# Windowed attention and a gated MLP on one core: six of nine token groups in blocks of two, the MLP's first product there by seven products of sums

## The chip, the cores and the metric

The kernel runs on one core of one Trainium2 chip. The metric is the device time of one execution in microseconds (us); lower is better. The engines are PE (matrix products), DVE (vectors), ACT (scalar functions and copies), POOL (a second, slower vector engine) and SP (issues nearly all the DMA transfers here). PE reads its operands from SBUF and writes to eight banks of PSUM, each of 128 partitions by 512 fp32.

## The reference

Eight batches, eight heads, 576 tokens, 64 values a head. Heads 0 to 3 attend to the last 32 tokens, heads 4 to 7 to every fourth of the last 128. The result, 4608 tokens by 512, goes through a gated MLP.

```python
scores = scale * np.matmul(q, k.transpose(0, 1, 3, 2))
scores = np.where(masks, scores, -1e9)          # window 32, or 32 of dilation 4
attn = exp(scores - max(scores)); attn = attn / (sum(attn) + 1e-9)
x = matmul(attn, v)                             # (B, S, H*D) -> 4608 x 512
h = x @ w_in                                    # 512 x 2048
g = h * (1.0 / (1.0 + np.exp(-1.702 * h)))
out = g @ w_out                                 # 2048 x 512
```

## The kernel before, in words

Every operand of the MLP's products is held as two fp32r parts, a high one and a low one; a product is three matmuls (high by high, low by high, high by low) of a 128x128 weight tile (stationary) by 128 x 512 tokens (moving). The weights arrive as 64-bit numbers and are decoded once on the chip: `decode(n)` fetches one of 32 tiles (16 of w_in, 16 of w_out) into one of five buffers called cells (L307, on SP's queue), and ACT, DVE and POOL turn it into a high and a low part (L311 to L321; the low part is a subtraction, L269). The names are wih, wil, woh and wol.

The tokens are worked through in nine groups of 512: m0 to m6 are the first 512 tokens of batches 0 to 6, r is the last 64 tokens of all eight batches, m7 the first 512 of batch 7; r comes before m7. For each group the MLP goes over 16 tiles f of d_ff. `up(f)` is the first product of one tile: 12 matmuls into one PSUM bank, hp (L631). Then ACT takes a tanh from the bank (L639), DVE multiplies it with the bank (the gate, L642), ACT copies the high part gh (L262) and DVE subtracts to get the low part gl (L269). `down(f)` is the second product of the tile, 12 matmuls (L667, L668, L671) into four banks acc0 to acc3, which hold the group's output over all 16 tiles. The second product of a tile follows the first product of the next, so the way from bank to gh and gl lies under matmuls.

Attention is done by head pairs, four to a batch, 32 in all, numbered k. A head pair is: scores on PE into the two banks sp (L408), mask, maximum and subtraction on DVE, exponential on ACT, sum and reciprocal on DVE, normalisation on POOL, transposes on DVE, eight copies into bt, then the product with v on PE (L509) into the bank av and the free end of sp, and copies from there into xm (the group's tokens) and xr (the rests). From the eighth head pair on the scores of the next pair and the product of this one are one piece on PE. The head pairs of a batch run while the group of the batch before is in the MLP. The first four run ahead of everything, and decoding runs through m0's stage.

No queue is written by hand. Each operation is added to a plan with its estimated cost on each engine that may do it, an urgency, and the names that it reads and writes; `Plan.ordered` then walks through estimated time and fixes the order on PE, ACT, DVE, POOL and SP's queue. An engine runs its instructions in that order, and so does SP's queue of transfers, where a transfer that waits for its data holds those behind it.

Of the kernel before, what the change touches and what calls it, by code (L numbers as in the profile page):

```python
# [7 lines left out]
F32 = mybir.dt.float32  # L8
# [13 lines left out]
LT = S - GT  # L22
AHEAD = 0.58
# [4 lines left out]
QT = 5  # L28
# [3 lines left out]
ROW = S // 4  # L32

# [130 lines left out]
def tile_windowed_attention_then_gated_mlp(  # L164
# [16 lines left out]
    ps = ctx.enter_context(tc.tile_pool(name="ps", bufs=1, space=bass.MemoryType.PSUM))  # L181
    plan = Plan()
# [14 lines left out]
    wih = fixed([P, NF, NC, P], F32R, "wih")  # L197
    wil = fixed([P, NF, NC, P], F32R, "wil")
    woh = fixed([P, NF, DM], F32R, "woh")
    wol = fixed([P, NF, DM], F32R, "wol")  # L200
    xh = fixed([P, NC, GT], F32R, "xh")
    xl = fixed([P, NC, GT], F32R, "xl")
    ghs, gls = ([fixed([P, GT], F32R, f"{n}{j}") for j in range(2)] for n in ("gh", "gl"))
    xm = fixed([P, NC, GT], F32, "xm")
    xr = fixed([P, B, NC, LT], F32, "xr")
# [29 lines left out]
    early = temp([P, GT], F32, "g32", "early")  # L235
# [32 lines left out]
    def pair(e, dst, a, b, op):  # L268
# [3 lines left out]
    second = fixed([P, 2, DM], U64, "second")  # L272
    cells = [temp([P, DM], U64, "ost", "cell0"), temp([P, DM], U64, "ost2", "cell1"), fixed([P, DM], U64, "cell2"),
             second[:, 0], second[:, 1]]
    words = fixed([P, 3, DM], U32, "words")

    def decode(n, urgency):
# [9 lines left out]
        if n % 2:  # L287
            src, hi, lo, key = w_out[f], woh[:, f], wol[:, f], f"wo{f}"
        else:
            hi, lo = (w[:, f].rearrange("p c n -> p (c n)") for w in (wih, wil))  # L290
            src, key = w_in[f], f"wi{f}"
# [37 lines left out]
    late, main_x, left_x = (t.rearrange(f"p {' '.join(d)} -> p ({' '.join(d)})") for t, d in (  # L329
        (second.bitcast(F32), "jn"), (xm, "cn"), (xr[:, 1:], "bcn")))  # L330
    nv = NW * D
    late_v = words.bitcast(F32).rearrange("p j n -> p (j n)")
# [4 lines left out]
    def lots(k):  # L337

        if 0 < k < NC:
            return f"first qk{k}", f"first v{k}"  # L340
        return ("qk0", "v0") if k < FIRST * NC or k % 2 == 0 else ("qk1", "v1")

    def load_qk(k):
        u, place = pairs[k], lots(k)[0]

        def work(e):
            if 0 < k < NC:
                flat = (None, late, main_x, left_x)[k]
            else:
                flat = late if place == "qk1" else temp([P, 2 * S], F32, "qk", f"qk_{k}")  # L350

            u["qk"] = flat[:, 0:2 * S]
            load(u["qk"], qk[k])
# [3 lines left out]
    def load_v(k):  # L357
        u, place = pairs[k], lots(k)[1]

        def work(e):  # L360
# [7 lines left out]
            flat = late_v if place == "v1" else temp([P, 2 * nv], F32, "v", f"v_{k}")  # L368
# [7 lines left out]
    def waits(k):  # L376

        if k >= FIRST * NC and k % 2:
            return [f"w{x}{f}" for x in "io" for f in range(NF - 3, NF)]
        return ["xh3.0"] if NC <= k < FIRST * NC else []  # L380
# [29 lines left out]

    def exponentials(k, urgency):
# [8 lines left out]
        if not masked(k):  # L420
            mine = mask if dilated(k) else plain
            for n, tiles, cost in ((P, slice(0, QT - 1), 0.62), (D, slice(QT - 1, QT), 0.22)):
                add({DVE: cost}, urgency, lambda e, n=n, tiles=tiles: pair(
                    e, pr[0:n, :, tiles], u["all"][0:n, :, tiles],
                    mine[0:n, None, tiles].broadcast_to([n, 2, tiles.stop - tiles.start, W]), ALU.add),
                    ("sp",), (PR,))
# [73 lines left out]
    def product(k):  # L500
        u = pairs[k]
        u["av"] = bank([P, GT], "av", f"av_{k}")
        sp = pairs[k + 1]["sp"] if k + 1 < len(pairs) else bank([P, 2, GT], "sp", f"sp_{k + 1}")
        u["rest"] = sp[:, 1, QT * W:QT * W + LT]
# [6 lines left out]
    def drain_x(k, urgency):  # L511
# [19 lines left out]
        if b == 0:  # L531
# [13 lines left out]
            for n, (part, src) in enumerate(rests):  # L545
                add({ACT: 0.22, DVE: 0.2}, urgency, lambda e, part=part, src=src: copy(e, part(xr[:, b, c]), src()),
                    FOUR, (f"xr{b}{c}.{n}",))
            return
        banks = ("av", "left")
        for n, (size, part, src, other) in enumerate(mains):  # L550
            place = banks[other]
            add({ACT: 0.12 + size * 0.001}, urgency, lambda e, part=part, src=src: copy(
                e, part(view(xm[:, c])), src()), (place,), (f"xm{c}.{n}", *freed))
        for n, (part, src, other) in enumerate(rests):
            add({ACT: 0.22, DVE: 0.2}, urgency, lambda e, part=part, src=src: copy(
                e, part(view(xr[:, b, c])), src()), (banks[other],),
                (f"xr{b}{c}.{n}", *(("first v3", "first qk3") if b == 1 else ())))
# [14 lines left out]
    def attention(k, urgency):  # L572


        def alone(j):
            add({PE: 1.6}, urgency - 1.0e5, lambda e: scores(j), (lots(j)[0], *(["mask"] if dilated(j) else [])), ("sp", "left", f"scores{j}"), 1.0)

        if k == NC:
# [3 lines left out]
        more, apart = k + 1 < len(pairs), k + 1 <= FIRST * NC  # L582
# [3 lines left out]
        if apart:  # L586
# [7 lines left out]
        ready = [f"scores{k + 1}"] if apart else [lots(k + 1)[0]] if more else []  # L594
        add({PE: 1.2 if apart or not more else 2.3}, urgency - 1.0e5, work,
            (lots(k)[1], *(f"bt.{m}" for m in range(8)), *ready), ("left", "av", *([] if apart else ["sp"])), 1.0)
        drain_x(k, urgency)

    class Group:


        def __init__(self, name, keys, dest):
            self.name, self.keys, self.dest = name, keys, dest
            self.g, self.acc, self.hps = {}, {}, {}
# [203 lines left out]
```

## Time and profile before

| | |
|---|---|
| median of 3 runs | 891.64 us (890.78 to 891.83) |
| span of the profiled execution | 888.8 us (the page gives no other time of it) |
| instructions | 17107, of them 7304 on PE |
| PE busy | 875.5 us, 99% of the span |
| DVE, ACT, POOL busy | 445.3, 392.4, 94.1 us |
| DMA | 61.32 MB, 69 GB/s on average |

The page is read from the busy times to the chain that ended last: the work followed back from the last instruction, at each step to what released it. In the rows of groups a form such as `hp_m<-xh,wih` names the tile written and the tiles read; m stands for any main group. In rows of a timeline a bracket at the end gives the idle time of the engine before the instruction, and what ended it. A matmul's duration in a timeline (0.39 us) is longer than its share of PE, because matmuls overlap; the distance between starts is what it costs. The rows are in the prediction.

### The profile page before, as it was taken

How to read it: one execution, taken by the hardware profiler on the slowest of the kernel's cores; microseconds unless marked ns; L12 is line 12 of the kernel's file. 1: busy time of each engine (PE TensorE's matmuls, PEld its weight loads, DVE VectorE, ACT ScalarE, POOL GpSimd, SP SyncE). 2: the span in 40 equal slices, each digit the busy share in tenths (PEclk: the TensorE clock that was granted, in tenths of full speed). 3: DMA queues.
4: the chain of work that ended last, by engine and by line, in shares of the span. 5: the costliest groups of instructions: out<-in, count | busy, mean ns of one | idle time of the engine just before them, and what ended most of it. 6: DMA issues, size and time to landing. Idle time of an engine off the chain costs nothing.

```text
span 888.8 us, 17107 instructions
## 1 busy us (share of the span) xinstructions
PE 875.5 (99%) x7304; PEld 715.8 (81%) x7304; DVE 445.3 (50%) x808; ACT 392.4 (44%) x687; POOL 94.1 (11%) x105
## 2 busy tenths in 40 slices
PE   6999999999999999999999999999999999999998
PEld 4678788888888888888888888888888888888886
DVE  6898986565556245543564265624522322232222
ACT  7898864443544245333543254424522332232222
POOL 3352331010101000000010010100100000000000
PEclk9899999999999999999999999999999999999999
DMA  9467752311231012200411023100100010002001
GB/s 360 149 204 227 223 140 95 94 48 47 96 94 48 0 56 87 88 8 0 142 47 48 1 95 94 48 1 26 44 1 1 0 48 1 1 0 48 1 1 47
DMA packets 35803, 61.32 MB, mean 69 GB/s; under 512 B 17424, under 2 KB 17680, under 8 KB 35728
## 3 DMA queue, kind: packets, MB, share of 16 engines
q1 hardware_dynamic: 35584, 60.11, 20.9%
q8 instruction: 57, 0.93, 0.5%
q14 instruction: 18, 0.15, 0.1%
q10 hardware_dynamic: 144, 0.13, 0.0%
HBM read 49.48 MB, written 9.44 MB: 66 GB/s over the span
## 4 chain that ended last, share of the span: by engine, by line
PE 97%; ACT 1%; DMA 1%; issue 0%; DVE 0%; SPq 0%
PE hp_m L631 40%; PE acc_m L667 13%; PE acc_m L671 13%; PE acc_m L668 13%; PE hp_r L631 5%; PE av L509 3%; PE sp L408 3%; PE acc_r L668 2%; PE acc_r L667 2%; PE acc_r L671 2%; DMA cell<-wo_dram 1%; PE first_x L495 1%; PE sp L509 0%; ACT cell L311 0%; ACT words L317 0%
## 5 line engine op out<-in xcount | busy, mean ns | idle before, releaser
L631 PE MATMUL hp_m<-xh,wih 128*128 128x512 f32 x512 | 202.2, 395 | 0.0
L667 PE MATMUL acc_m<-gh,woh 128*128 128x512 f32 x512 | 200.6, 392 | 0.0
L631 PE MATMUL hp_m<-xl,wih 128*128 128x512 f32 x512 | 199.7, 390 | 0.4 <-DVE xl L269 0.4
L631 PE MATMUL hp_m<-xh,wil 128*128 128x512 f32 x512 | 199.8, 390 | 0.0
L668 PE MATMUL acc_m<-gh,wol 128*128 128x512 f32 x512 | 199.3, 389 | 0.0
L642 DVE SCALAR_TENSOR_TENSOR g_m<-g_m,hp_m 128x512 f32<-128x512 f32 x128 | 87.7, 686 | 214.4 <-ACT g_m L639 213.4
L639 ACT ACTIVATE g_m<-hp_m 128x512 f32<-128x512 f32 x128 | 76.8, 600 | 234.3 <-PE hp_m L631 233.8
L671 PE MATMUL acc_m<-gl,woh 128*128 128x512 f32 x512 | 142.5, 391 | 0.0
L269 DVE TENSOR_TENSOR gl<-g_m,gh 128x512 fp32r<-128x512 f32 x126 | 92.5, 734 | 61.3 <-ACT gh L262 59.2
L631 PEld LDWEIGHTS hp_m<-xh,wih 128*128 128x128 f32 x512 | 96.4, 188 | 21.3
L631 PEld LDWEIGHTS hp_m<-xl,wih 128*128 128x128 f32 x512 | 96.4, 188 | 21.2 <-DVE xl L269 0.9
L667 PEld LDWEIGHTS acc_m<-gh,woh 128*128 128x128 f32 x512 | 96.1, 188 | 20.6
L262 ACT ACTIVATE gh<-g_m 128x512 fp32r<-128x512 f32 x126 | 79.8, 633 | 73.3 <-DVE g_m L642 73.1
L668 PEld LDWEIGHTS acc_m<-gh,wol 128*128 128x128 f32 x512 | 96.1, 188 | 19.6
L631 PEld LDWEIGHTS hp_m<-xh,wil 128*128 128x128 f32 x512 | 96.4, 188 | 19.1
L671 PEld LDWEIGHTS acc_m<-gl,woh 128*128 128x128 f32 x512 | 95.5, 188 | 20.1
L269 POOL TENSOR_TENSOR pr<-pr,sm 128x320 f32<-128x320 f32 x64 | 49.4, 793 | 312.5 <-DVE sm L437 312.5
L262 ACT ACTIVATE bt<-ct 32x320 f32<-32x320 f32 x100 | 46.9, 469 | 5.1 <-DVE ct L458 3.2
L262 ACT ACTIVATE xm<-av 128x512 f32<-128x512 f32 (+2 forms) x42 | 24.5, 592 | 47.6 <-PE av L509 25.1
L269 POOL TENSOR_TENSOR xl<-xm,xh 128x512 fp32r<-128x512 f32 x10 | 13.8, 1394 | 260.0 <-ACT xh L262 256.3
L431 ACT ACTIVATE pr<-pr 128x640 f32<-128x640 f32 x32 | 23.7, 740 | 29.2 <-DVE pr L269 29.0
L642 DVE SCALAR_TENSOR_TENSOR g_r<-g_r,hp_r 128x512 f32<-128x512 f32 x16 | 11.0, 688 | 49.7 <-ACT g_r L639 49.7
(125 smaller groups left out, 850.7 us busy)
## 6 DMA issues: line engine op xcount, KB each, us to landing
qk<-qk_dram SPq DMA_DIRECT2D x17, 576.0 KB, 4.5
out_dram<-ost_m SPq DMA_DIRECT2D x31, 256.0 KB, 2.1
second<-qk_dram SPq DMA_DIRECT2D x13, 576.0 KB, 4.3
v<-vp_dram SPq DMA_DIRECT2D x32, 216.0 KB, 4.5
words<-vp_dram SPq DMA_DIRECT2D x24, 216.0 KB, 4.4
cell<-wi_dram SPq DMA_DIRECT2D x10, 512.0 KB, 4.7
cell<-wo_dram SPq DMA_DIRECT2D x9, 512.0 KB, 4.7
second<-wo_dram SPq DMA_DIRECT2D x6, 512.0 KB, 4.9
```

The costliest lines, as they stand in the source:

```text
L262: A.activation(dst, src, AF.Copy, scale=scale)
L269: (V if e == DVE else G).tensor_tensor(out=dst, in0=a, in1=b, op=op)
L408: T.matmul(dst[:, w:w + n], u["qk"][rows, at:at + 32], u["qk"][rows, S + first:S + first + n], start=not masked(k), stop=True, tile_positi ...
L431: add({ACT: 0.75}, urgency, lambda e: A.activation(prs[y], prs[y], AF.Exp, scale=0.125), (), (PR,))
L495: T.matmul(u["x"][D * a:D * a + D, g, at:to], u["v"][32 * g:32 * g + 32, s - 1 if dilated(k) else s, a], ct[32 * g:32 * g + 32, a, n:n + t ...
L509: T.matmul(dst, u["v"][a][0:KW, m], bt[0:KW, a, m], start=True, stop=True, skip_group_check=True)
L631: T.matmul(hps[f], st[:, f, c], mv[:, c], start=c == 0 and k == 0, stop=c == NC - 1 and k == 2)
L639: A.activation(self.g32, hps[f], AF.Tanh, scale=0.851)
L642: V.scalar_tensor_tensor(out=self.g32, in0=self.g32, scalar=1.0, in1=hps[f], op0=ALU.add, op1=ALU.mult)
L667: T.matmul(self.acc[j], woh[:, f, cols], gh, start=f == 0, stop=False)
L668: T.matmul(self.acc[j], wol[:, f, cols], gh, start=False, stop=False)
L671: T.matmul(self.acc[j], woh[:, f, P * j:P * j + P], self.g[f][1], start=False, stop=f == NF - 1)
```

## The change

Groups m0, m1 and m2 stay as they were. The other six are taken in three blocks of two: p (batches 3 and 4), q (batches 5 and 6) and r (the rests, then batch 7).

In a block, two tiles of d_ff, f = u and f = u + 8, are made together for both groups: a 2 by 2 block product over the two halves of d_model, by the scheme of Strassen in the form with seven products. With weights' sums (index b) and tokens' sums (index a) the seven are listed in `PRODUCTS`; each is 6 matmuls (two chunks of d_model by three parts). They alternate between the banks hp and av; some of them are added up in PSUM, three results are copied out to SBUF and come back as an addition on DVE. The first group's gated tiles are multiplied with w_out at once, in 16 pieces spread between the seven products of the next pair; the second group's are kept in SBUF, and their 16 steps of the second product come after the block's eight pairs (`rest`).

- Weights' sums: `sum_weights(u)` makes four sums for each pair u, with high and low parts, and writes them and three plain parts to DRAM (`sums`, 56 tiles of 256 KB). Every product of every block loads its tile into one of eight slots (168 loads of 256 KB).
- Tokens' sums: tokens of batches 3 to 7 and the rests are written to DRAM (L587, L599) and loaded per block (L842, eight tiles); `sum_tokens` adds and splits them, and the parts take the place of w_in in SBUF.
- w_out of f from 9 on is written to DRAM once (`outs`, 7 tiles of 512 KB) and loaded again in turns (18 loads).
- Buffers: cells, tokens, gated values and output tiles share an array of 22 units, `arena`. Attention has one buffer for q and k and one for v instead of two.
- Attention is moved earlier, since the first block needs two batches at once: head pairs 8 to 11 and the next ones run in m1's stage, up to 22 in m2's, and the last, 31, in the fifth pair of block p. Scores and products are always separate pieces on PE now, and from head pair 20 on the product goes into the banks sp.

The core of the diff:

```diff
-        more, apart = k + 1 < len(pairs), k + 1 <= FIRST * NC
+        more = k + 1 < len(pairs) and k + 1 != INNER
...
-        def work(e):
-            if more and not apart:
-                scores(k + 1)
-            product(k)
...
+        add({PE: 1.25}, urgency - 1.0e5, lambda e: product(k),
+            (lots(k)[1], *(f"bt.{m}" for m in range(8)), *([f"scores{k + 1}"] if more else [])),
+            ("sp",) if k >= INNER else ("left", "av"), 1.0)
...
+    def sum_weights(u):
+        f, g = u, u + PAIRS
...
+        for n, (w, cols) in enumerate(((f, half[0]), (f, half[1]), (g, half[1]))):
+            add({DMA: 262}, urgency, lambda e, n=n, w=w, cols=cols: load(
+                sums[7 * u + n].rearrange("p (h n) -> p h n", h=2), f32(wi(w)[:, :, cols])), (f"wi{w}",), (f"sums{u}.{n}",))
...
+        add(add_costs, urgency, lambda e: both(e, b1, f), (f"wi{f}",), own(6))
+        add(add_costs, urgency, lambda e: both(e, b2, g), (f"wi{g}",), own(7))
...
+        add({DMA: 1049}, urgency, lambda e: load(
+            sums[7 * u + 3:7 * u + 7].rearrange("i p (h n) -> p h i n", h=2), parts_), ...)
+    PRODUCTS = ((0, 0), (3, 1), (4, 2), (2, 3), (5, 4), (1, 5), (6, 6))
...
+        def product(self, u, n, place, fresh):
+            b, a = PRODUCTS[n]
+            slot = ring[0] % (2 * NC)
...
+            add({DMA: 262}, -3.0, lambda e: load(f32(xs[:, slot]), sums[7 * u + b]), (f"sums{u}.{b}",), (key, *extra))
+            def work(e, c):
...
+                for k, (st, mv) in enumerate(((0, 0), (1, 0), (0, 1))):
+                    at = 2 * P * st + P * c
+                    T.matmul(self.banks[place], xs[:, slot, at:at + P], wi_kept[:, 2 * a + c, mv], ...)
+        def up(self, u):
+            X, Y = ("hp", "av") if u % 2 == 0 else ("av", "hp")
...
+            share = -(-len(pending) // 7)
+            self.product(u, 0, X, True)
+            copied(X, s1)
+            some(share)
+            self.product(u, 1, Y, True)
+            copied(Y, s5)
+            some(share)
+            self.product(u, 2, X, False)
+            copied(X, u2)
+            some(share)
+            self.product(u, 3, Y, False)
+            plus(Y, u2, h12)
+            gated(lambda: unit(h12), (f"A{h12}",), 6, h12, own(h12))
+            some(share)
+            self.product(u, 4, X, False)
+            plus(X, s5, gg)
+            gated(lambda: unit(gg), (f"A{gg}",), 5, gg, own(gg))
+            some(share)
+            self.product(u, 5, Y, True)
+            plus(Y, s1, h11)
+            gated(lambda: unit(h11), (f"A{h11}",), 6, h11, own(h11))
+            some(share)
+            self.product(u, 6, X, False)
+            gated(lambda: banks[X], (X,), 5, gf, own(gf))
+            some(len(pending))
+            pending.extend(first(h12, g, 1))
+            pending.extend(first(h11, f, 0))
+        def rest(self):
+            for n, f in enumerate(self.second_order):
+                at, y = GATED[f], n % 2
+                split(lambda at=at: unit(at), ghs[y], gls[y], (f"A{at}",), (f"gh{y}", f"gl{y}"), -9.5)
+                for piece in self.downs[1].pieces(f, ghs[y], gls[y], (f"gh{y}", f"gl{y}")):
+                    piece()
```

The order on three engines, at the places that the prediction speaks of.

SP's queue in m0's stage, before: fetches of cells (L307) with attention's transfers between them (L472 moves transposed probabilities into bt, L371 loads v).

```order
L307 DMA cell0_114<-wo_dram 128x512
L472 DMA bt_86<-ct0_84 32x10x32 x8
L307 DMA cell1_115<-wi_dram 128x512
L307 DMA cell2_116<-wo_dram 128x512
L307 DMA second_113<-wi_dram 128x512
L371 DMA v_5_1100<-vp_dram 96x576 x2
L307 DMA second_113<-wo_dram 128x512
```

The same place after (L332 is the fetch, L794 the write of a plain part of w_in to `sums`):

```order
L332 DMA arena_77<-wo_dram 128x512
L496 DMA bt_90<-ct0_88 32x10x32 x8
L332 DMA arena_77<-wo_dram 128x512
L794 DMA sums_78<-wi_kept_68 256x1x256 x3
L332 DMA arena_77<-wi_dram 128x512
L794 DMA sums_78<-wi_kept_68 256x1x256
L394 DMA v_5_1113<-vp_dram 96x576 x2
L332 DMA arena_77<-wo_dram 128x512
```

The writes of weights' parts now stand between the fetches; in m0's stage there are 14 such places ahead of a fetch.

PE in the middle of a group, before: the end of a first product into the bank hp, and the second product of the tile before it.

```order
L631 MATMUL hp_m5_8_5767<-xh_70,wih_66 128x512
L631 MATMUL hp_m5_8_5767<-xh_70,wil_67 128x512
L631 MATMUL hp_m5_8_5767<-xl_71,wih_66 128x512
L667 MATMUL acc_m5_0_5322<-gh1_73,woh_68 128x512
L668 MATMUL acc_m5_0_5322<-gh1_73,wol_69 128x512
L667 MATMUL acc_m5_1_5328<-gh1_73,woh_68 128x512
```

After, the end of the fourth pair of block q and the start of its fifth (L877 is a product of sums, named by pair and by the first product in its bank; qa is the block's first group, L682 its low parts by w_out):

```order
L877 MATMUL up_q_3_0_6188<-wi_kept_68,xs_72 128x512 x6
L682 MATMUL acc_qa_0_6006<-gl0_75,wo_kept_70 128x512
L682 MATMUL acc_qa_1_6011<-gl0_75,wo_kept_70 128x512
L682 MATMUL acc_qa_2_6015<-gl0_75,wo_kept_70 128x512
L877 MATMUL up_q_3_5_6263<-wi_kept_68,xs_72 128x512 x6
L682 MATMUL acc_qa_3_6026<-gl0_75,wo_kept_70 128x512
L877 MATMUL up_q_3_0_6188<-wi_kept_68,xs_72 128x512 x6
L877 MATMUL up_q_4_0_6283<-wi_kept_68,xs_72 128x512 x6
L678 MATMUL acc_qa_0_6006<-gh1_74,wo_kept_70 128x512
```

The sixth product fills a bank (up_q_3_5), and the next pair's first product (up_q_4_0) takes the same bank seven matmuls later.

DVE over one tile, before, a gate and a low part:

```order
L642 SCALAR_TENSOR_TENSOR g32_m6_9_6518<-g32_m6_9_6518,hp_m6_9_6503 128x512
L269 TENSOR_TENSOR gl1_75<-g32_m6_9_6518,gh1_73 128x512
L642 SCALAR_TENSOR_TENSOR g32_m6_10_6548<-g32_m6_10_6548,hp_m6_10_6533 128x512
L269 TENSOR_TENSOR gl0_74<-g32_m6_10_6548,gh0_72 128x512
L642 SCALAR_TENSOR_TENSOR g32_m6_11_6578<-g32_m6_11_6578,hp_m6_11_6563 128x512
```

After, over one pair of tiles of block q (L297 is an addition out of a bank, or a low part; L909 the gate; wi_last_units is a place in SBUF where the second group's gated values stay):

```order
L297 TENSOR_TENSOR arena_77<-up_q_3_1_6208,arena_77 128x512
L909 SCALAR_TENSOR_TENSOR arena_77<-arena_77 128x512
L297 TENSOR_TENSOR wi_last_units_4828<-up_q_3_0_6188,arena_77 128x512
L297 TENSOR_TENSOR gl1_76<-arena_77,gh1_74 128x512
L909 SCALAR_TENSOR_TENSOR wi_last_units_4828<-arena_77,wi_last_units_4828 128x512
L297 TENSOR_TENSOR arena_77<-up_q_3_5_6263,arena_77 128x512
L909 SCALAR_TENSOR_TENSOR arena_77<-arena_77 128x512
L909 SCALAR_TENSOR_TENSOR wi_last_units_4828<-arena_77,up_q_3_0_6188 128x512
L297 TENSOR_TENSOR gl0_75<-arena_77,gh0_73 128x512
```

For a tile of one group DVE had two instructions; for two tiles of two groups it has nine here, and the additions, which free a bank, stand behind gates that read SBUF alone.

More of the change, by code (lines that the diff above doesn't have):

```diff
@@ L418, in sp @@
             return u["all"] if masked(k) else pr
[L420 to L426, printed above, removed]
+        if FIRST * NC <= k < INNER:
+            add_mask(k, urgency)
         add({DVE: 0.80}, urgency, lambda e: V.tensor_reduce(out=mx, in_=sp(), axis=AX.X, op=ALU.max),
@@ L741, in tile_windowed_attention_then_gated_mlp @@
                     decode(n, 25.0 + 2.3 * n)
-            if last:
-                last[0].down(last[1])
-            last = g, f
-        nxt += g in main
-    last[0].down(last[1])
+    held.update({f: f for f in range(KEPT, NOUT)})
+    for n, block in enumerate(blocks):
+        turns.extend(block.first_order + block.second_order)
+    for n, block in enumerate(blocks):
+        block.sum_tokens()
+        for b in (5 + 2 * n, 6 + 2 * n):
+            if b < B:
+                for c in range(NC):
+                    attention(NC * b + c, 1000.0 * b + c)
+        for u in range(PAIRS):
+            block.up(u)
+        some(len(pending))
+        block.rest()
     def warm(i):
```

411 lines of the change are left out of this document (294 added, 117 removed).

## The prediction

> **What bounds the kernel now.** I read the page's busy times first, then the chain that ended last, then the table of stretches.
>
> ```profile
> span 888.8 us, 17107 instructions
> PE 875.5 (99%) x7304; PEld 715.8 (81%) x7304; DVE 445.3 (50%) x808; ACT 392.4 (44%) x687; POOL 94.1 (11%) x105
> PE 97%; ACT 1%; DMA 1%; issue 0%; DVE 0%; SPq 0%
> PE hp_m L631 40%; PE acc_m L667 13%; PE acc_m L671 13%; PE acc_m L668 13%; PE hp_r L631 5%; PE av L509 3%; PE sp L408 3%; PE acc_r L668 2%; PE acc_r L667 2%; PE acc_r L671 2%; DMA cell<-wo_dram 1%; PE first_x L495 1%; PE sp L509 0%; ACT cell L311 0%; ACT words L317 0%
> ```
>
> PE is busy 99% of the span and makes 97% of the chain; 45% of the chain is the MLP's first product (L631) and about 45% the second (L667, L668, L671). A busy PE can still be a slow one, so the stretches come next. Columns: stretch, length, then busy time and count of PE, weight load, DVE, ACT, POOL, granted clock, DMA share, GB/s.
>
> ```profile
> 38.00:889.00 851.00, 846.55 (x6468) 696.64 (x6468) 417.70 (x745) 361.34 (x643) 78.98 (x83) 1.00 0.19 61
> 60.00:150.00 90.00, 90.00 (x817) 72.99 (x816) 77.68 (x133) 69.15 (x117) 28.39 (x25) 1.00 0.58 176
> 245.00:340.00 95.00, 95.00 (x779) 78.55 (x768) 47.54 (x89) 39.02 (x72) 7.37 (x9) 1.00 0.17 56
> 70.00:80.00 10.00, 10.00 (x143) 7.83 (x142) 9.53 (x18) 9.27 (x16) 0.84 (x3) 1.00 0.89 301
> 90.00:100.00 10.00, 10.00 (x142) 7.95 (x137) 10.00 (x17) 9.60 (x16) 2.91 (x3) 1.00 0.84 272
> ```
>
> After the first 38 us PE is idle for 4.5 us in all, at a granted clock of 1.00. The two 10 us stretches show the hardest case: DVE at 95% and 100%, ACT at 93% and 96%, DMA at 301 and 272 GB/s, and PE at 10.00 of 10. So nothing there slows PE, and the pace of its instructions prices the change. The chain gives it, from that busy stage and from a quiet one:
>
> ```profile
> 85.67 2.72 PE hp_m L631 x12
> ...
> 268.91 2.72 PE hp_m L631 x12
> ```
>
> 2.72 / 12 = 0.2267 us for a 128x128 by 128x512 matmul in both stages.
>
> **The change, part by part.** Removed: a pair of d_ff tiles for two groups took 2 x 2 x 12 = 48 first-product matmuls and takes 7 x 6 = 42. Three blocks of eight pairs make 3 x 8 x 6 = 144 matmuls fewer, 144 x 0.2267 = **-32.65 us**. All of it lies on PE, so all of it counts as long as PE stays fed.
>
> Scores and products of attention stand apart on PE now. Before, from the eighth head pair on, the scores of the next pair and the product of this one were one piece. What each way takes is read from the starts of the matmuls around it (start, duration; "..." hides rows of the same piece and one L667):
>
> ```profile
> 114.10 0.39 PE L631 MATMUL hp_m<-xl,wih 128*128 128x512 f32 x1
> 114.42 0.97 PE L408 MATMUL sp<-qk 64*32 64x64 f32 x72
> ...
> 115.65 0.39 PE L668 MATMUL acc_m<-gh,wol 128*128 128x512 f32 x1
> ...
> 121.58 0.39 PE L668 MATMUL acc_m<-gh,wol 128*128 128x512 f32 x1
> 121.90 1.15 PE L509 MATMUL av<-bt,v 96*64 96x64 f32 x32
> ...
> 123.44 0.39 PE L668 MATMUL acc_m<-gh,wol 128*128 128x512 f32 x1
> ...
> 139.78 0.39 PE L668 MATMUL acc_m<-gh,wol 128*128 128x512 f32 x1
> 140.10 0.97 PE L408 MATMUL sp<-second 64*32 64x64 f32 x72
> ...
> 142.54 0.40 PE L668 MATMUL acc_m<-gh,wol 128*128 128x512 f32 x1
> ```
>
> Between the first and last start of each stand two big matmuls, 0.45 us. Scores alone cost 115.65 - 114.10 - 0.45 = 1.10, a product alone 123.44 - 121.58 - 0.45 = 1.41, both in one piece 142.54 - 139.78 - 0.45 = 2.31. Apart is 0.20 dearer; 23 head pairs were merged before and none is now: **+4.5 us**. The rest of attention is only moved to earlier stages.
>
> The results' way out. Before, a tile of the first product had one bank and one chain, tanh (ACT), gate (DVE), high part (ACT), low part (DVE), under a second product of 12 matmuls:
>
> ```profile
> 873.28 0.39 PE L631 MATMUL hp_m<-xl,wih 128*128 128x512 f32 x1
> ...
> 873.71 0.60 ACT L639 ACTIVATE g_m<-hp_m 128x512 f32<-128x512 f32 x1 [3.46 <-PE hp_m L631]
> ...
> 874.34 0.69 DVE L642 SCALAR_TENSOR_TENSOR g_m<-g_m,hp_m 128x512 f32<-128x512 f32 x1 [3.36 <-ACT g_m L639]
> ...
> 875.06 0.63 ACT L262 ACTIVATE gh<-g_m 128x512 fp32r<-128x512 f32 x1 [0.75 <-DVE g_m L642]
> ...
> 875.73 0.69 DVE L269 TENSOR_TENSOR gl<-g_m,gh 128x512 fp32r<-128x512 f32 x1 [0.70 <-ACT gh L262]
> ...
> 876.23 0.39 PE L631 MATMUL hp_m<-xh,wih 128*128 128x512 f32 x1
> ```
>
> The bank was free at 874.34 + 0.69 = 875.03 and wanted at 876.23: 1.2 us to spare. A pair of tiles now takes 42 + 24 = 66 matmuls, 66 x 0.2267 = 14.96 us of PE, and for it DVE has 3 additions, 4 gates and 2 low parts, 9 x 0.69 = 6.2 us, ACT 3 copies, 4 tanh and 2 high parts, 9 x 0.61 = 5.5 us: both under half. But two banks alternate over seven products, and the gaps are unequal. The tightest is from the sixth product's end to the next pair's first, in the same bank: seven matmuls, 1.59 us, for an addition of about 0.95 us from PE's end to DVE's end (873.28 + 0.39 to 873.71 is 0.04, so 0.04 + 0.69 and a turn of the semaphores). If one gate of 0.69 stands ahead of it on DVE, it still just fits. The next tightest is 12 matmuls, 2.72 us, for the last product's tanh and gate, 0.04 + 0.60 + 0.03 + 0.69 = 1.4 us with no queue. Without attention these hold. In the first block, where attention's vector work (instructions of up to a microsecond) runs through five pairs, three such turns a pair can be late. Ends: 0, if all fit, and 5 x 3 x 0.8 = 12 us, if each comes an instruction late. I take **+2.5 us**, near the lower end, since PE lost nothing in the stretch 60 to 150 with the same one-bank turn and DVE at 86%.
>
> Vector work of the weights' and tokens' sums. Per head pair the stretch 245 to 340 has 4 of them and about 85 / 5.44 = 15.6 tiles of 1.42 us: (47.5 - 22.2) / 4 = 6 us of DVE. From the second group's start to the first block's fifth pair PE has 174 + 75 + 23 x 2.5 = 306 us of work; DVE has 32 tiles x 1.42 = 45, 5 pairs x 6.2 = 31, 23 head pairs x 5.7 to 6 = 131 to 138, about 16 for the weights' sums with half of them on POOL, 12 for the tokens' sums, about 240 us: 78%, below the 86% under which PE was never late. Cost 0; if the cover fails it is the second rival.
>
> DMA. 168 loads of weights' sums of 256 KB, one per product, and 56 sums written; all on SP's queue.
>
> ```profile
> out_dram<-ost_m SPq DMA_DIRECT2D x31, 256.0 KB, 2.1
> qk<-qk_dram SPq DMA_DIRECT2D x17, 576.0 KB, 4.5
> ...
> SPq L353 <- PE sp L408: 358.3, 25, 46.5
> SPq L307 <- DVE words L269: 25.2, 12, 8.9
> ```
>
> A transfer of 256 KB lands in 2.1 us (row 1; estimate for a load of the same size), and eight slots let it be issued seven products, about 15 us, ahead. In steady state that is covered; cost 0. SP is in order, though: row 3 is its wait for attention's buffers, up to 46.5 us, row 4 the fetch of the next weight cell for a buffer that decoding has not yet freed, 25.2 us in 12 waits. Writes of sums stand among the fetches of the first stage now, each waiting for its weights' low part; behind it wait the later fetches, and decoding, and at last PE. How much slack there is shows where a decoded tile meets its use:
>
> ```profile
> 110.52 0.68 DVE L269 TENSOR_TENSOR wil<-words,wih 128x512 fp32r<-128x512 f32 x1
> ...
> 111.76 2.73 PE hp_m L631 x12
> ...
> 116.81 0.69 DVE L269 TENSOR_TENSOR wil<-words,wih 128x512 fp32r<-128x512 f32 x1
> ...
> 118.80 2.72 PE hp_m L631 x12
> ```
>
> The 14th tile is ready at 111.20 for 111.76 (0.56 us), the 15th at 117.50 for 118.80 (1.3 us). Ends: 0, if the five cells' lead swallows the waits, and 6 us, if three waits of 25.2 / 12 = 2.1 us come through. I take **+2 us**. Last, in a block's second half the first split waits for the last product of the half before; in two blocks the next block's pulled-ahead product covers it, in the last nothing does: 873.71's ACT row and one turn, **+0.6 us**.
>
> Sum: -32.65 + 4.5 + 2.5 + 2 + 0.6 = -23 us. The profiled execution spans 888.8 us, 2.84 below the median of 891.64 (the page gives no other time of it); the sum is a difference, so I set it on the median: 891.6 - 23 = **868 us**. What a measurement here tells from no change is 0.2%, 1.8 us.
>
> [...] DVE and POOL disturb each other in the trace: with a POOL subtraction running, a DVE one takes 1.31 us, alone 0.68.
>
> ```profile
> 92.70 0.68 DVE L269 TENSOR_TENSOR wol<-words,woh 128x512 fp32r<-128x512 f32 x1
> ...
> 96.60 1.32 POOL L269 TENSOR_TENSOR words<-words,cell 128x512 uint32<-128x512 uint32 x1 [4.97 <-ACT cell L311]
> 97.16 1.31 DVE L269 TENSOR_TENSOR wol<-words,woh 128x512 fp32r<-128x512 f32 x1
> ```
>
> [...]
>
> **The rivals.**
>
> 1. The two banks' turns bind in the first block: 12 us in place of 2.5, 878 us. For: three turns under 3 us a pair. Against: the free time of 1.2 us before was never exceeded.
> 2. DVE and POOL work one at a time and become the bound. POOL has about 92 us in the stretch of 306 (before, 28.39 of 90 from 60 to 150); 240 + 92 = 332, +25 us: 893 us, no change. Against: 77.68 + 28.39 = 106 us of both fitted into 90 us there, so they do overlap, and PE lost nothing. [...]
> 3. Slower: SP's queue in the first stage. The writes of sums come in 14 places ahead of weight fetches. If each holds its fetch by the 2.1 us of the row above and none is caught up, +29 us: 868 - 2 + 29 = 895. It decides from 12 of the 14 on (23 / 2.1 = 11). For: slack of 0.56 and 1.3 us. Against: a write waits for a tile decoded earlier than the one that frees the cell, and decoding lives off five cells.
> 4. Sums' loads come late in the first block, where SP stands behind attention's loads (row 3 of the queue): some 8 head pairs there x 2.1 us = 17, 885 us. Against: the lead of 15 us.
>
> **How the numbers follow.** The forecast has 0.73, the rivals 0.12, 0.04, 0.06 and 0.05. Faster: 0.73 + 0.12 + 0.05 = 0.90; same 0.04 (rival 2); slower 0.06 (rival 3). The lower end has the three uncertain costs at their lowest, 891.6 - 32.65 + 4.5 - 0 = 863, and 2 us for a shorter start, 861. Upward, rival 1 with the start at its 6 us is 882; 880 leaves out rivals 2 to 4 and a little of rival 1, under 0.2.
>
> **What would show it.** The pace: a product of six matmuls takes 1.36 us and a pair without attention 15.0 us in the chain; at 16 us each turn is late. Idle time of PE in the blocks with an addition (L297) or a gate (L909) as releaser is rival 1; with a load of sums, rival 4. In the first stage, PE's idle time before L631 with a decoding instruction as releaser, and long waits of SP for the low parts, are rival 3; the third group should begin within 2 to 6 us of before. DVE over 95% with PE below 95% in the second and third group is rival 2. I would be wrong altogether if the matmuls on sums ran slower than 0.2267 us, or if the granted clock fell under the added transfers.

## The result, and the profile after

The changed kernel takes 876.79 us (median of 4 runs, 876.05 to 877.82); the kernel before 891.74 (median of 4). The ratio is 0.9837 (95% interval 0.9823 to 0.9851): 1.6% faster, 15 us where 23 were forecast. 876.79 lies inside the range (861 to 880), 8.8 us above the forecast of 868.

The page after, the rows of busy times and of the chain that ended last:

```profile
span 876.1 us, 17851 instructions
PE 853.5 (97%) x7160; PEld 688.8 (79%) x7160; DVE 521.6 (60%) x923; ACT 450.8 (51%) x789; POOL 148.8 (17%) x156
PE 88%; DMA 7%; DVE 2%; ACT 2%; issue 1%; SPq 0%; DVEq 0%; ACTq 0%
```

PE's share of the chain fell from 97% to 88%, and 7% is DMA now. PE is idle for 22.6 us (876.1 - 853.5) instead of 13.3 (888.8 - 875.5). Where this stands is read from the starts of each group's first matmul in the traces:

| stage | before, us | after, us |
|---|---|---|
| start to the first matmul of m0 | 25.5 | 26.9 |
| m0 | 105.0 | 116.2 |
| m1 | 101.0 | 104.2 |
| m2 | 96.3 | 109.2 |
| the rest | 561.1 | 519.7 |

m1 and m2 hold more head pairs than before, so their growth is moved work. m0 holds one piece of scores more than before (72 matmuls, 1.10 us at the prediction's price) and otherwise the same work on PE, and it is 11.1 us longer. The stretch 40 to 130 lies inside it; before (first fence) and after, columns as in the prediction:

```profile
40.00:130.00 90.00, 90.00 (x855) 72.35 (x854) 83.48 (x142) 78.81 (x131) 30.96 (x26) 1.00 0.67 205
```

```profile
40.00:130.00 90.00, 83.07 (x785) 65.46 (x784) 75.84 (x136) 73.91 (x121) 28.39 (x23) 0.99 0.87 281
```

Where most of PE's 7 idle us lie, in stretches of 10 us after:

```profile
80.00:90.00 10.00, 7.54 (x33) 5.61 (x32) 7.67 (x15) 9.04 (x15) 2.08 (x2) 1.00 0.75 226
...
110.00:120.00 10.00, 8.82 (x107) 6.77 (x106) 7.41 (x15) 7.15 (x16) 0.10 (x1) 1.00 1.02 365
120.00:130.00 10.00, 7.18 (x28) 5.53 (x27) 6.99 (x14) 6.93 (x11) 3.57 (x2) 0.89 0.80 264
130.00:140.00 10.00, 10.00 (x102) 7.74 (x101) 7.22 (x13) 5.78 (x14) 3.09 (x3) 0.93 0.51 182
```

PE is idle for 2.5, 1.2 and 2.8 us in them. DVE, ACT and POOL are each below 91% there, and the share of the transfer engines is 0.75, 1.02 and 0.80. The granted clock, the third number from the end, falls to 0.89 and 0.93 after the last hole: it is half (0.50) for 3.4 us from 127.9 on. The chain at the last hole (start, duration) goes back to fetches of weights:

```profile
107.00 4.66 DMA arena<-wo_dram
...
114.75 9.33 DMA arena<-wo_dram
...
124.66 0.65 ACT arena L342
125.31 1.23 ACT arena L336
126.54 0.43 ACT arena L777
...
127.00 0.70 DVE arena L778
...
127.74 4.62 PE hp_m L769 x12
```

A fetch of a w_out tile took 9.33 us; decoding (L342, L336 on ACT) began late, the tanh (L777) and the gate (L778) of the tile before stood behind it, and PE waited for the bank. The transfers of the window 40 to 130, before and then after:

```profile
DMA packets 15871, 18.42 MB, mean 205 GB/s; under 512 B 11362, under 2 KB 11362, under 8 KB 15859
q1 hardware_dynamic: 15859, 18.26, 66.2%
...
cell<-wo_dram SPq DMA_DIRECT2D x6, 512.0 KB, 4.7
```

```profile
DMA packets 21417, 25.33 MB, mean 281 GB/s; under 512 B 11692, under 2 KB 16552, under 8 KB 21406
q1 hardware_dynamic: 21406, 25.19, 86.0%
...
arena<-wo_dram SPq DMA_DIRECT2D x11, 512.0 KB, 6.2
...
sums<-wi_kept SPq DMA_DIRECT2D x18, 256.0 KB, 5.8
```

6.9 MB more pass in the same 90 us, the engines' share goes from 66% to 86%, a fetch of w_out lands after a median of 6.2 us instead of 4.7, and the writes of sums themselves need 5.8 us, where a quiet output store of the same size took 2.1 before.

The blocks, on the other hand, ran as reckoned. The stretch of block p's five pairs with attention, and one pair of block q:

```profile
356.44:449.72 93.28, 93.04 (x1147) 74.39 (x1146) 67.44 (x137) 61.48 (x118) 17.09 (x20) 1.00 0.78 248
553.17:568.12 14.95, 14.95 (x67) 12.40 (x66) 6.92 (x10) 5.62 (x10) 1.28 (x1) 1.00 0.43 127
```

A pair takes 14.95 us (forecast 14.96), and the five pairs under attention leave PE idle for 0.24 us (a wait of scores for their q and k, at 363 us).

### The profile page after: what moved, and what is told of

Same layout as the page of the kernel before. It is cut to its first block, busy times and chain, and to the rows that moved or that the text cites. A ratio compares the mean times of both kernels' runs of the same rounds, so it can differ in the third digit from the quotient of the medians.

```text
span 876.1 us, 17851 instructions
## 1 busy us (share of the span) xinstructions
PE 853.5 (97%) x7160; PEld 688.8 (79%) x7160; DVE 521.6 (60%) x923; ACT 450.8 (51%) x789; POOL 148.8 (17%) x156
## 4 chain that ended last, share of the span: by engine, by line
PE 88%; DMA 7%; DVE 2%; ACT 2%; issue 1%; SPq 0%; DVEq 0%; ACTq 0%
PE hp_m L769 13%; PE up_r L877 9%; PE up_p L877 8%; PE up_q L877 8%; PE acc_m L678 4%; PE acc_m L682 4%; PE acc_m L679 4%; PE av L537 3%; PE sp L429 3%; DMA qk<-qk_dram 2%; DMA arena<-wi_dram 2%; PE acc_pa L678 2%; PE acc_pa L682 2%; PE acc_rb L678 2%; PE acc_pa L679 2%; PE acc_rb L682 2%
## 5 line engine op out<-in xcount | busy, mean ns | idle before, releaser
L769 PE MATMUL hp_m<-xs,wi_kept 128*128 128x512 f32 x504 | 129.1, 399 | 4.1 <-DVE arena L778 3.6
L769 PEld LDWEIGHTS hp_m<-xs,wi_kept 128*128 128x128 f32 x504 | 93.6, 190 | 26.2 <-DVE arena L778 5.3
L297 DVE TENSOR_TENSOR gl<-arena,gh 128x512 fp32r<-128x512 f32 x108 | 78.8, 730 | 48.8 <-ACT gh L290 23.6
L290 ACT ACTIVATE gh<-arena 128x512 fp32r<-128x512 f32 x109 | 68.9, 632 | 56.3 <-DVE arena L909 15.8
L877 PE MATMUL up_p<-wi_kept,xs 128*128 128x512 f32 x336 | 86.8, 394 | 0.0
L877 PE MATMUL up_r<-wi_kept,xs 128*128 128x512 f32 x336 | 83.3, 390 | 0.0
L877 PE MATMUL up_q<-wi_kept,xs 128*128 128x512 f32 x336 | 83.3, 390 | 0.0
L297 POOL TENSOR_TENSOR pr<-pr,sm 128x320 f32<-128x320 f32 x64 | 51.7, 825 | 153.4 <-DVE sm L461 138.7
L877 PEld LDWEIGHTS up_q<-wi_kept,xs 128*128 128x128 f32 x336 | 63.1, 188 | 13.0
L877 PEld LDWEIGHTS up_r<-wi_kept,xs 128*128 128x128 f32 x336 | 63.1, 188 | 13.0
L877 PEld LDWEIGHTS up_p<-wi_kept,xs 128*128 128x128 f32 x336 | 62.4, 188 | 13.4
L678 PE MATMUL acc_m<-gh,wo_kept 128*128 128x512 f32 x156 | 62.5, 400 | 0.0
L679 PE MATMUL acc_m<-gh,wo_kept 128*128 128x512 f32 x156 | 60.9, 390 | 0.0
L909 DVE SCALAR_TENSOR_TENSOR arena<-arena 128x512 f32<-128x512 f32 x57 | 41.3, 724 | 25.1 <-ACT arena L908 25.0
L297 POOL TENSOR_TENSOR arena<-arena 128x256 f32<-128x256 f32 (+2 forms) x43 | 40.2, 947 | 57.4 <-DVE arena L297 24.4
L297 POOL TENSOR_TENSOR wi_kept<-arena,wi_kept 128x512 fp32r<-128x512 f32 x14 | 19.9, 1423 | 172.4 <-PE up_q L877 102.1
L777 ACT ACTIVATE arena<-hp_m 128x512 f32<-128x512 f32 x48 | 28.9, 601 | 34.2 <-PE hp_m L769 34.0
L778 DVE SCALAR_TENSOR_TENSOR arena<-arena,hp_m 128x512 f32<-128x512 f32 x48 | 32.9, 686 | 18.8 <-ACT arena L777 18.5
L682 PE MATMUL acc_m<-gl,wo_kept 128*128 128x512 f32 x156 | 42.5, 393 | 0.0
L297 DVE TENSOR_TENSOR arena<-up_q,arena 128x512 f32<-128x512 f32 x19 | 13.1, 689 | 49.2 <-PE up_q L877 49.1
```

The lines of the kernel that those rows point to most:

```text
L290: A.activation(dst, src, AF.Copy, scale=scale)
L297: (V if e == DVE else G).tensor_tensor(out=dst, in0=a, in1=b, op=op)
L678: T.matmul(self.acc[j], w[:, 0, cols], high, start=f == self.order[0], stop=False)
L679: T.matmul(self.acc[j], w[:, 1, cols], high, start=False, stop=False)
L682: T.matmul(self.acc[j], w[:, 0, P * j:P * j + P], low, start=False, stop=f == self.order[-1])
L769: T.matmul(hps[f], wi(f)[:, st, cols], mv[:, c], start=c == 0 and k == 0, stop=c == NC - 1 and k == 2)
```

## The experiments

Three theories for the 11 us of m0's stage. *Bytes*: the added writes share the transfer engines with the fetches. *Queue*: a write that waits for its data holds the fetches behind it on SP. *Moved attention*: work pulled into m0 and the single buffer for q and k.

**Writes after m0.** Each write in the plan also reads a name that m1's split of tokens writes:

```diff
...
-  f32(wi(w)[:, :, cols])), (f"wi{w}",), (f"sums{u}.{n}",))
+  f32(wi(w)[:, :, cols])), (f"wi{w}", "xh0"), (f"sums{u}.{n}",))
...
-                    (f"wo{f}",), (f"outs{f}",))
+                    (f"wo{f}", "xh0"), (f"outs{f}",))
```

> The changed kernel with the 24 plain parts of the weights' sums and the 7 tiles of w_out written to DRAM only after m0's stage, nothing else changed by hand. Bytes (the writes crowd the transfers of m0's stage, so that weights land late): m0's stage is 103 to 106 us long as before instead of 116, the time 866 +- 2 us. Queue (the writes hold the fetches behind them in SP's queue): the same 866, so this run doesn't part the two. Attention moved ahead and its single buffer as cause: 875 to 877, m0's stage stays at 114 to 116.

Measured: 870.96 us, ratio to the kernel before 0.9773 (0.9758 to 0.9788); m0's stage 105.7 us. Its stretch 40 to 130, and two of m1, where the writes now begin together:

```profile
40.00:130.00 90.00, 90.00 (x921) 71.96 (x921) 83.50 (x142) 78.87 (x131) 30.36 (x26) 1.00 0.69 213
```

```profile
130.00:160.00 30.00, 28.96 (x224) 23.18 (x223) 25.55 (x43) 16.48 (x29) 12.72 (x13) 1.00 1.05 368
...
180.00:200.00 20.00, 18.26 (x235) 14.43 (x236) 14.96 (x24) 9.95 (x20) 11.12 (x13) 0.91 0.60 186
```

The writes are the cause of m0's loss: with the same pieces on PE the stage is 10.5 us shorter than in the changed kernel, within 0.6 us of before. Moved attention is not the cause: DVE does more in the stretch than in the changed kernel (83.5 us against 75.8), with PE at 90.00 of 90. But only 6 us came out at the end, and the 866 that was expected is missed. m1 lost some 4.5 us: 1.0 idle under transfers at 1.05 and 368 GB/s, 1.7 idle later with transfers at 0.60, and about 1.7 of clock (3.4 us at half; 0.91 in the second row). So bytes need not be all of m1's loss.

**An eighth at the old place.** Each write is split by partitions, 0 to 15 where it was and 16 to 127 after m0 (the writes of w_out are split in the same way):

```diff
+ for part, size, need, key in ((slice(0, 16), 33, (), "first"), (slice(16, P), 229, ("xh0",), "")):
+     add({DMA: size}, urgency, lambda e, ...: load(sums[7 * u + n, part]..., f32(wi(w)[part, :, cols])),
+         (f"wi{w}", *need), (f"sums{u}.{n}{key}",))
...
```

> As the changed kernel, but of each of those writes only 16 of 128 partitions go at the old place in SP's queue; the other 112 follow after m0's stage. The waits in the queue stay, an eighth of the bytes stays. Bytes: within 2 us of the run with all writes after m0 (866 to 868). Queue: 875 to 877, as the changed kernel, with SP's waits before the writes as long as there.

Measured: 872.92 us (0.9795, 0.9778 to 0.9811); m0's stage 106.9 us. Its stretch, and SP's waits between 40 and 133 (total, times, longest):

```profile
40.00:130.00 90.00, 89.82 (x920) 71.81 (x918) 83.09 (x141) 78.77 (x131) 30.00 (x26) 1.00 0.73 219
```

```profile
SPq L795 <- POOL wi_kept L297: 2.9, 1, 2.9
SPq L795 <- DVE wi_kept L297: 2.7, 3, 1.4
SPq L999 <- DVE wo_kept L297: 2.2, 1, 2.2
```

The three rows are the longest; in all SP waits 12.2 us ahead of the writes in m0's stage, against 16.0 in the changed kernel, and PE is idle for 0.18 us. So it is the bytes; the waits in the queue and the eighth that stayed cost at most some 1.2 us of m0 together (106.9 against 105.7). The whole time is 2.0 us above the run before, at the edge of what was expected: m1 has 3.5 us of idle PE here, where that run has 2.8.

**The kernel before with the writes added.**

```diff
+        if g is main[1]:
+            for u in range(8):
+                for n, (w, part) in enumerate(((u, wil), (u, wih), (u + 8, wil))):
+                    add({DMA: 262}, 2500.0 + 10.0 * u, lambda e, ...: load(sums[3 * u + n], ...), (f"wi{w}",), ...)
+            for f in range(9, NF):
+                for n, part in enumerate((woh, wol)):
+                    add({DMA: 262}, 2600.0, lambda e, ...: load(outs[2 * f + n], f32(part[:, f])), (f"wo{f}",), ...)
```

> The kernel before with writes of the same kind and size (24 and 14 of 256 KB, to scratch that nobody reads), put into the plan as the change does, and nothing else. Bytes or queue: +7 to +11 us on the kernel before (899 to 903), with PE idle in m0's stage. Attention moved ahead as cause: 891 to 893.

Measured: 898.23 us, 1.0080 (1.0065 to 1.0095), +7.1. m0's stage is 110.0 us against 105.0 with the same pieces on PE, and the start is 2.2 us later (the start moves by up to 1.8 us between runs without such writes too, so that part isn't shown to come from them). The stretch 40 to 130:

```profile
40.00:130.00 90.00, 85.77 (x828) 67.79 (x828) 78.64 (x139) 76.88 (x122) 31.34 (x25) 1.00 0.86 285
```

So the writes do harm without the rest of the change. The same share of the transfer engines, about 0.86, costs m0 4.9 us here, and the writes cost 10.5 in the changed kernel. 1.7 us of the difference is the stretch of 3.4 us at half the clock there; the remaining 4 or so were not separated. The two are not quite the same load: the added writes go in packets of 1 KB in the changed kernel (4860 packets between 512 B and 2 KB from 40 to 130 us); here no packet lies between these sizes.

**Joint pieces of scores and product again** (on top of the first run):

```diff
...
+        joint = more and FIRST * NC <= k and k + 1 < INNER
+        if more and not joint:
+            alone(k + 1)
+        def work(e):
+            if joint:
+                scores(k + 1)
+            product(k)
...
```

> As the run with all writes after m0, and scores of the next head pair and product of this one in one piece on PE again for the eleven head pairs 8 to 18. If the piece's price is all there is (2.30 us joint, 1.10 + 1.40 apart): 11 x 0.2 = 2.2 us less than that run, 864. If joint pieces keep the next scores from running ahead of the product so that attention isn't ready for the first block: PE idle before the first block, 2 to 10 us more than that run.

Measured: 877.5 us, 0.9846 (0.9832 to 0.9861), 6.5 more than the run it is built on. m1 is 9.8 us shorter (4.5 of it that run's loss) and m2 8.4, since head pairs are left over, and p with them is 26.1 longer. The start of p (stretches, then PE's waits in p):

```profile
340.00:350.00 10.00, 4.89 (x92) 3.01 (x86) 8.59 (x14) 5.38 (x12) 1.27 (x1) 0.63 0.69 220
350.00:360.00 10.00, 9.27 (x90) 6.92 (x91) 7.59 (x14) 4.70 (x9) 2.69 (x3) 0.51 0.46 135
```

```profile
PE up_p L885 <- ACT arena L290: 3.5, 2, 2.8
PE sp L429 <- DMA qk<-qk_dram: 2.3, 1, 2.3
```

The block waits for its tokens, and some 17 us pass at half the clock (by the 0.63 and 0.51 of the two rows, 7.4 + 9.8). Separate pieces are dearer on PE, by 0.20 us a head pair in the prediction's rows, and here they are what lets attention be done in time.

**The kernel before with separate pieces** (`more = apart = k + 1 < len(pairs)`).

> The kernel before with scores and products as separate pieces throughout and nothing else. By the price of the pieces (2.30 joint, 2.50 apart, 23 times): +4.6 us, 895.7. If separate pieces also let attention run ahead, that brings nothing here, since PE waited for no attention before: the same 895.7. If the two are worth each other: 891.

Measured: 896.61 us, 1.0059 (1.0042 to 1.0076), +5.2 against 891.44 (3.7 to 6.8 by the interval): the price of the pieces, with nothing given back.

**Writes spread over m1.** Three plain parts after each even tile of m1, a w_out tile after each odd one:

```diff
...
+            if b == 1 and f % 2 == 0:
+                plain_parts(f // 2, "gl0")
+            if b == 1 and f % 2 and f < 14:
+                w = KEPT + f // 2
+                add({DMA: 524}, 2600.0, lambda e, f=w: load(outs[f]..., f32(wo(f))), (f"wo{w}", "gl1"), (f"outs{w}",))
```

> The changed kernel with the writes of the weights' plain parts and of w_out spread over m1's stage, three or one after each tile of d_ff, in place of m0's stage (or m1's start, as in the first run of this study). If only the crowding of transfers was lost, at both places: m0's stage 105 to 106 us, no idle PE in m1, 865 to 867 us. If the loss moves on with the bytes wherever they go: 870 or more.

Measured: 870.18 us, 0.9761 (0.9747 to 0.9776), no better than the first run by the intervals. m0's stage is 106.2 us, but PE is still idle for 2.5 us in m1, in two holes. Transfers are not full there (0.67 and 0.85), so their share alone doesn't explain it:

```profile
131.00:160.00 29.00, 27.97 (x250) 22.24 (x249) 25.01 (x42) 18.66 (x34) 15.94 (x17) 1.00 0.67 224
160.00:200.00 40.00, 38.54 (x433) 30.42 (x433) 30.52 (x50) 22.87 (x47) 20.89 (x25) 1.00 0.85 273
```

DVE is busy for 86% of the first stretch (25.01 of 29) and POOL for 55%. The rows of both engines ahead of the second hole show more:

```profile
166.95 3.63 POOL L297 TENSOR_TENSOR arena<-wi_kept 128x512 f32<-128x512 f32 x2
167.65 1.78 DVE L297 TENSOR_TENSOR gl<-arena,gh 128x512 fp32r<-128x512 f32 x1
169.35 1.78 DVE L292 CAST arena<-arena 128x1024 fp32r<-128x1024 f32 x1
...
172.65 0.68 DVE L778 SCALAR_TENSOR_TENSOR arena<-arena,hp_m 128x512 f32<-128x512 f32 x1
...
173.39 0.96 PE L769 MATMUL hp_m<-xs,wi_kept 128*128 128x512 f32 x3 [1.46 <-DVE arena L778]
```

Beside two POOL additions a low part and a cast take 1.78 us each on DVE; elsewhere the same low part takes 0.69 (at 174.03), and the cast takes 0.69 in the next run. The gate that frees PE's bank stands behind them: 2.2 us lost on DVE ahead of a hole of 1.46.

**Sums without POOL** (on top of that; the last two pairs of lines are the differences of the weights' sums and their low part):

```diff
...
-    add_costs = {DVE: -0.70, POOL: 1.36}
+    add_costs = {DVE: -0.70}
...
-            add({DVE: -0.40, POOL: 0.75}, urgency, ...
+            add({DVE: -0.40}, urgency, ...
...
-        add({DVE: -1.25, POOL: 2.6}, urgency, ...
+        add({DVE: -1.25}, urgency, ...
```

> As the run with the writes spread, but the additions, differences and the low part of the weights' sums, and the additions of tokens, may go to DVE only, none to POOL. If DVE and POOL exclude each other in these instructions, POOL's share bought nothing: same time within 1 us, and PE without idle time in m1 and m2. If POOL relieved DVE: DVE near 90% in m1 and m2 and PE idle there, 3 to 10 us more.

Measured: 866.88 us, 0.9723 (0.9709 to 0.9738), 3.3 us less than with POOL on the same chip, where the same time within 1 us or a longer one was expected. The same stretches:

```profile
131.00:160.00 29.00, 29.00 (x322) 23.19 (x321) 26.50 (x50) 17.12 (x32) 5.10 (x6) 1.00 0.65 217
160.00:200.00 40.00, 40.00 (x377) 32.39 (x370) 35.15 (x71) 20.82 (x41) 4.27 (x6) 1.00 0.86 285
```

m1's idle time is gone, with DVE at 91% of the first stretch (26.50 of 29), so DVE's share alone had not made the holes. (The plan also put one product of attention into m2 instead of m1 here.) The busy times of the whole page, with POOL and without, show the exchange:

```profile
PE 851.2 (98%) x7160; PEld 686.8 (79%) x7160; DVE 524.8 (60%) x922; ACT 452.0 (52%) x793; POOL 142.6 (16%) x153
```

```profile
PE 851.2 (98%) x7160; PEld 686.5 (79%) x7160; DVE 529.4 (61%) x958; ACT 452.8 (52%) x796; POOL 106.3 (12%) x114
```

POOL lost 36.3 us, and DVE, with 36 instructions more, has only 4.6 more. The 32 differences alone are 13.1 us of DVE work (m1's groups by form, sums without POOL, first row); many of the others became shorter, and some longer. The low parts of gated values in m1, with POOL (second fence) 828 ns, without 714:

```profile
L297 DVE TENSOR_TENSOR arena<-arena 128x256 f32<-128x256 f32 x32 | 13.1, 408 | 0.1
L297 DVE TENSOR_TENSOR gl<-arena,gh 128x512 fp32r<-128x512 f32 x16 | 11.4, 714 | 0.6 <-ACT gh L290 0.5
```

```profile
L297 DVE TENSOR_TENSOR gl<-arena,gh 128x512 fp32r<-128x512 f32 x17 | 14.1, 828 | 2.8 <-ACT gh L290 2.8
```

So 36.3 us of work on POOL bought 4.6 us of time on DVE: beside POOL's instructions some of DVE's took longer, 1.78 us against 0.69 in the rows above; why is not shown. POOL's work alone does not make the loss: the changed kernel, with the writes in m0, has no idle PE in m1 with as much of it (17.73 of the 29 us from 143 to 172, DVE at 81%), and neither has the run with joint pieces, which has writes and POOL's sums there but fewer head pairs. Which share each has when they meet was not separated.

**The changed kernel with that alone** (writes in m0 as they were).

> The changed kernel with its writes where they are (in m0's stage), and the sums' arithmetic on DVE only, none on POOL. If the crowded transfers of m0's stage and the exclusion of DVE by POOL in m1 are two separate losses: m0's stage 114 to 117 us as in the changed kernel, no idle PE after it, 874 to 877 us. If POOL's part was behind m0's loss too: m0's stage under 110 us, 868 to 871.

Measured: 875.34 us, 0.9819 (0.9806 to 0.9833). m0's stage stays long, 112.6 us, so POOL's sums are not behind most of m0's loss. It lies between the two values expected, though: 3.6 us shorter than in the changed kernel, with PE idle for 5.2 us of it instead of 7.4 and no stretch at half the clock (the granted clock of the profiled execution is 0.994 on average, 0.992 in the changed kernel), and why was not followed up. The whole time is no better than the changed kernel's by the intervals. There was no loss in m1 to take away, since PE has no idle time there with POOL's sums either.

**All low parts without POOL too** (on top of the spread writes and the sums without POOL, also the splits of tokens and gated values).

> As the run with writes spread and sums without POOL, and also the low parts of tokens and gated values on DVE only (POOL keeps the normalisation of attention and part of the decoding). If POOL's work only delays DVE: DVE's busy time grows by less than the 20 to 25 us that POOL loses, PE without idle time, 865 to 867 us. If POOL still relieves DVE there: DVE over 90% in m1 and m2, PE idle, 868 to 872.

Measured: 866.98 us, 0.9727 (0.9714 to 0.9740), the same as with the sums alone taken from POOL. POOL has 82.3 us and DVE 538.8: 24 us less for 9.4 more, and PE had no idle time left to win in m1 and m2.

**Two slots for the loads of sums** (on top of the spread writes; `slot = ring[0] % 2`).

> As the run with the writes spread, but the loads of weights' sums go to two slots instead of eight, so that a load can start only when the product two before is done: a lead of about one product and its pieces, 2.1 us, for a landing of 2 to 3 us. If the lead of eight slots is what hides the loads: 168 loads late by 0.3 to 1 us, 50 to 150 us more. If the loads were hidden anyway: no change.

Measured: 919.34 us, 1.0296 (1.0255 to 1.0336), 49 us more than with eight. The two largest of PE's waits, and the loads (count, KB, median us to landing, 500 to 600):

```profile
PE up_p L880 <- DMA xs<-sums: 10.8, 9, 2.0
PE up_r L880 <- DMA xs<-sums: 8.5, 8, 2.0
```

```profile
xs<-sums SPq DMA_DIRECT2D x22, 256.0 KB, 2.6
```

The blocks are 16.4, 14.5 and 17.6 us longer. PE is idle for some 30 us more in them (30.2 by its waits for loads of sums and for gates), and two stretches of 3.4 us at half the clock fall into them (0.988 on average over the profiled execution, 0.992 with eight slots); the rest of the 49 us was not separated. The lead of eight slots is what makes the 168 loads free.

## Why the prediction was right, and which term was mis-sized

- **The matmuls, -32.65 us.** Right. A pair takes 14.95 us, six matmuls 1.36 us, and 144 are gone (7304 - 7160).
- **Separate pieces, +4.5 us.** Right in size: the kernel before with separate pieces alone measured +5.2. What the sum lacked was their use: with joint pieces the changed kernel loses 6.5 us.
- **The two banks' turns, +2.5 us (0 to 12).** Too high. p's five pairs left PE idle for 0.24 us, and not for a bank. The first rival (0.12) didn't happen; the busy stretch 60 to 150 of the kernel before was the right row to go by. The prediction's 0.95 us for an addition was an estimate, with a turn of some 0.2 us that no row showed; in block q one ends 0.75 us after PE's last matmul (566.70 to 567.45).
- **SP's queue in m0, +2 us (0 to 6).** This is the term that failed: m0 grew by 11.1 us, of which 1.1 is a moved piece of scores, and 10 is above the upper end. The place was right (the third rival's), the mechanism wasn't. I priced the writes as waits in the queue, at most three of 2.1 us; the transfers themselves had no price. I didn't add up their bytes: some 6.9 MB, in a stage that already kept the transfer engines at 66%. The row of 301 GB/s with PE at 10.00 was read as proof that such a rate does no harm. The rate as such does none in the changed kernel either (373 GB/s from 50 to 60 us with PE at 10.00); the harm is that fetches land later, and PE's holes begin at 81 us. Slack of 0.56 and 1.3 us at the 14th and 15th tile, quoted there, was the warning.
- **The last block's uncovered split, +0.6 us.** Measured 0.75, from start to start less one matmul (827.70 - 826.72 - 0.23). The copy of the high part starts beside the last matmul of the half before, right behind three copies of that half's output on ACT; which of the two held it is not shown.

```profile
825.56 1.58 ACT L290 ACTIVATE arena<-acc_ra 128x512 f32<-128x512 f32 x3 [1.41 <-PE acc_ra L682]
...
826.72 0.39 PE L682 MATMUL acc_ra<-gl,wo_kept 128*128 128x512 f32 x1
...
827.00 0.64 ACT L290 ACTIVATE gh<-arena 128x512 fp32r<-128x512 f32 x1
...
827.70 0.19 PEld L678 LDWEIGHTS acc_rb<-gh,wo_kept 128*128 128x128 f32 x1 [1.01 <-ACT gh L290]
```

- **Vector work at nothing.** Right for the changed kernel: from the second group's start to the fifth pair of p (143.07 to 449.72, 306.65 us where 306 were reckoned) PE is idle for 0.24 us, with DVE at 75% (78% reckoned; (47.5 - 22.2) / 4 in that reckoning is 6.3, not 6). That POOL's work delays DVE's, the second rival's ground, showed by 3.3 us (870.18 against 866.88) once the writes stood in m1.
- **Loads of sums at nothing.** Right, and the two slots show what it hung on.

One sign named ahead could not be read as it stood: the third group begins 15.9 us later than before, not 2 to 6, but 3.3 of it is m1 with more head pairs in it.

That the time still lies inside the range is in part luck. The room above the forecast had been reckoned from the banks' turns, which cost next to nothing, and SP's queue in m0, 4 us above its own upper end, used it up.

In the profiled executions: -32.65 + 4.6 (23 x 0.2) + 0.2 + 10.0 (m0 without the moved scores) + 0.75 = -17.1, and the start was 1.4 later: -15.7. The spans differ by -12.7; the 3 us left were not traced. The medians differ by 15.0, since the profiled execution of the changed kernel was the longest of its four (877.82 us) and that of the kernel before, by its span, one of its shorter ones. The start is no term of the change: it lies between 25.8 and 27.6 us in the seven runs built on the changed kernel that have no writes of full size in m0.

## What to carry to other kernels

When transfers are added to a stage, add up its bytes against what its transfer engines already carry, not only the places in the queue: at a share of 0.66 PE lost nothing here, at 0.86 the fetches took 1.3 times as long to land (a median of 6.2 us against 4.7) and PE waited. Moving the writes to a stage without weight fetches gave 6 us back; spreading them there gave no more by the intervals. Work put on POOL should be tried on DVE alone: here 36 us of POOL bought DVE 4.6, and taking it away gave 3.3 us (866.9, the best time here, against 870.2) where the writes stood in m1, and nothing clear of noise where they stood in m0.

## What the runs showed of the hardware that was not expected

After some holes in PE's work the granted clock fell to half for a while, and the loss outlasted the hole: 2.8 us idle in m0 and then 3.4 us at half the clock in the changed kernel (0.50 from 127.9 to 131.3), 1.7 idle in m1 and then 3.4 at half with the writes after m0 (0.91 over the 20 us from 180 on), and in the run with joint pieces some 17 us at half in p (0.63 and 0.51 in the stretches above; 0.984 on average over the execution, 0.992 in the changed kernel). Not every hole did it: one of 1.9 us in m0 in the run with the writes in place and no POOL sums and one of 1.7 us in m1 in the run with an eighth in place were followed by none (both executions have 0.994 on average, as has the kernel before, which is at 1.00 from 38 us on). What decides is not shown. From 350 to 360 us in the run with joint pieces PE is busy for 9.27 of 10 us at a clock of 0.51, so its busy time alone would not have shown that stretch as a slow one.
